# A transformer block on one core: Wo and reciprocal loads over 128 partitions, the last q tile around the shift products, chunk 1's scaling in another order

## Chip, cores and metric

One NeuronCore of a Trainium2 chip. The engines are TensorE (PE), VectorE (DVE), ScalarE (ACT), GpSimd (POOL) and SyncE (SP), which here only issues DMAs. SBUF has 128 partitions, PSUM 8 banks of 128 x 512 float32. The time is the device time of one execution in microseconds (us); the figure given is a median of runs.

## What is computed

A block with adaptive layer norm, linear attention with 32 heads of 32, and a SwiGLU feed-forward part. S = 2048 rows, D = 1024, F = 3584, everything bfloat16. Cut to what matters:

```python
mod = silu(c) @ w_mod                      # six rows of D: sa, ca, ga, sb, cb, gb
h = layernorm(x) * (1 + ca) + sa
q, k, v = split_heads(h @ wqkv)
phi = lambda t: where(t > 0, t + 1, exp(t)) + 1e-06
pq, pk = phi(q), phi(k)
kv = einsum('bhsd,bhse->bhde', pk, v)
z = einsum('bhsd->bhd', pk)
o = einsum('bhqd,bhde->bhqe', pq, kv) / (einsum('bhqd,bhd->bhq', pq, z) + 1e-06)
x = x + ga * (o @ wo)
h = layernorm(x) * (1 + cb) + sb
x = x + gb * ((silu(h @ w_gate) * (h @ w_up)) @ w_down)
```

## The kernel before

The program is one list of operations that the Python code writes out by hand. Each engine runs its own operations in the order in which they were written; a helper (L176) records every operation and works out the semaphore waits between engines from the SBUF bytes and the PSUM banks that each one touches. For PSUM the rule is by whole banks: an operation waits for the last operation of every other engine on its bank. So most lines of the profile carry L176, and instructions are told apart by tile names: `ps` is PSUM, `ht` the transposed and normalised input (two buffers of 8 x 128 x 512), `wqk` the q and k weights, `e`/`rl` and `e1x`/`rlx` the slots for exp and relu, `pqt` and `pkt`/`pk` the finished phi(q) and phi(k), `wo` the output weights, `rb` the reciprocal denominators copied to the partitions of their heads.

The rows of x are worked on in four chunks of 512.

**Chunk 0's q phase** (`q_phase_chunk0`) runs while weights still arrive. Seven of the eight q tiles (nt 0 to 6) grow in seven banks at once, one input tile dt after another (`q_part`), since the scale columns (`mod_sc` with WCA) and shift columns (`mod_sc` with WSA) of the modulation come out of PE in between. For dt 0 to 3 (and dt 4 and 5 in the first seven tiles) the shift isn't added to HT in time; its product with the weights is made separately (`bias_mm`) and added as a bias (`bias_fin` copies it to BIASQ) when ACT takes exp and relu of a tile (`q_phi`). Bank 0 holds those modulation columns, so the eighth tile (nt 7) is made at the end, in bank 0, after `bias_fin`; `h0_shift` then adds the shift to HT for the k products. DVE meanwhile does layer norm statistics of chunk 1 (x tiles 4 to 7; tile 4 by two ACT passes, `act_stats`, and `act_var`), normalises them (`ln1_xn`, `ln1_xn_sum`), and SP sends each through a DMA transpose into HT's second buffer (`th_dma`). `q_min` and `q_add` turn exp and relu into phi(q).

**k groups of chunk 0, then chunks 1 to 3.** `k_group` and `q_group` each make 8 products of 128 x 512 into a bank taken from `next_bank`; `phi_evac` takes exp on ACT, and for each pair of groups `phi_flush` finishes on DVE. `kside` hangs other work behind the k groups of chunk 0: behind group 1 the scaling of chunk 1's HT (`th_mod(1, ...)`, 16 halves of 256 columns) and then the last two q tiles; behind groups 3 and 4 ACT's statistics for tiles 10 and 11.

**G, M and Wo.** For 16 groups `g_group(g)` multiplies phi(k) with the normalised x into five banks (`G_BANKS`); `g_evac` takes a group out on ACT and DVE one group later. Behind g = 0, `z_row` is made, and SP issues ZB's broadcast and the loads of Wo: two calls of `wo_load`, each four DMAs, each with 32 partitions of WO (L938). Behind g = 1, `den` makes the denominators, DVE inverts them into RCB (partition 32 x chunk + head), SP writes them to DRAM in four DMAs, waits, and reads them back in eight DMAs, each filling 32 partitions of RB for four head groups (L988). The first four are awaited together (lane rb0), the next four together (rb1). On DVE `fold_ga` multiplies Wo by ga (g = 6 to 9) and `scale_pq(hg)` multiplies phi(q) by RB (g = 7 to 14), each behind the `g_evac` of its step. `kvt_mm` and `m_mm` form kv and its product with Wo (MW), half 0 behind g = 10 to 12, half 1 after the groups; `wo_part` then multiplies phi(q) by MW. Bank 2 is the bank of G group 14 and also of the first `wo_part`.

The feed-forward part follows and is untouched.

Of the kernel before, what the change touches and what calls it, by code (L numbers as in the profile page):

```python
# [5 lines left out]
FP32 = mybir.dt.float32  # L6
# [256 lines left out]
def bass_adaLN_cond__linear_attn_block__swiglu_ffn__prompt_kernel(  # L263
# [16 lines left out]
    NCH = 4  # L280
# [5 lines left out]
    with ExitStack() as es:  # L286
# [59 lines left out]
        RL = T("rl", 188 * KB, [128, 4, 512], BF16)  # L346
        E1X = T("e1x", 192 * KB, [128, 4, 512], BF16)
        RLX = T("rlx", 196 * KB, [128, 4, 512], BF16)
        ACC = T("acc", 192 * KB, [128, D], FP32)
        MHL = T("mhl", 196 * KB, [128, 2, D], BF16)  # L350
        MHLT = T("mhlt", 192 * KB, [128, 2 * NDT, 128], BF16)
# [351 lines left out]
        def next_bank():  # L703
            i = qk_ctr[0]
            qk_ctr[0] += 1
            return (1, 2, 3, 4, 6, 7, 5, 0)[i % 8] if i < 40 else i % 5 + 1

        def q_group(ch, nt):
            buf, bank = ch % 2, next_bank()
# [39 lines left out]
        def mod_row_b(bank, i, dst):  # L749
# [3 lines left out]
            P.wait_for("sp", [wr])  # L753
            P.dma("mdr%d" % i, dst[:], MDR[i].unsqueeze(0).to_broadcast([128, D]))

        def q_slot(nt):
            return (E1, RL) if nt < 4 else (E1X, RLX)

        def q_phi(nt, bank):
            for buf, fn_ in zip(q_slot(nt), (ACT.Exp, ACT.Relu)):  # L760
                P.act("activation", out=buf[:, nt % 4, :], in_=PS[:, bank, :], func=fn_, bias=BIASQ[:, nt:nt + 1])

        def q_min(nts):
            for nt in nts:
                e = q_slot(nt)[0][:, nt % 4, :]
                P.dve("tensor_scalar", out=e, in0=e, scalar1=1.0, scalar2=1e-6, op0=ALU.min, op1=ALU.add)

        def q_add(nts):
            for nt in nts:
                e, r = q_slot(nt)  # L770
                P.dve("tensor_tensor", out=PQT[:, nt, 0:512], in0=r[:, nt % 4, :], in1=e[:, nt % 4, :], op=ALU.add)

        def q_phase_chunk0():
            qb = [1, 2, 3, 4, 6, 7, 5]
            fin_ca(2, 2)
            for dt in (2, 3):
                h0_first(dt, "dve")
            for nts, dts in ((range(3), (0,)), (range(3), (1,)), ((3, 4, 5, 6), (0, 1))):
                for nt in nts:
                    q_part(nt, qb[nt], dts)  # L780
            for nt in range(7):
                if nt == 4:
                    mod_sc(WCA, 8, range(4, 8))
                    fin_ca(4, 4)
                    for dt in (4, 5):
                        h0_scale_only(dt)
                q_part(nt, qb[nt], (2, 3))
            act_stats(4, (0,))
            for nt in range(7):
                if nt == 6:  # L790
                    mod_sc(WSA, 0, range(6, 8))
                    fin_sa(6, 2)
                    for dt in (6, 7):
                        h0_scale(dt)
                q_part(nt, qb[nt], (4, 5))
            mod_sc(WSA, 0, range(4, 6))
            fin_sa(4, 2, True)
            for dt in (4, 5):
                h0_shift(dt)
            for nt in range(7):  # L800
                if nt == 2:
                    bias_mm((4, 5))
                q_part(nt, qb[nt], (6,))
            for nt in range(7):
                if nt == 1:
                    mod_sc(WSA, 0, range(4), range(4))
                if nt == 3:
                    mod_sc(WSA, 0, range(4), range(4, 8))
                    fin_sa(0, 4, True)
                    ln_ops[1][0]()  # L810
                if nt == 5:
                    bias_mm(range(4))
                    bias_fin()
                q_part(nt, qb[nt], (7,))
            ln_ops[1][1]()
            ln_ops[1][2]()
            ln1_rstd1(5)
            for i, dt in enumerate((4, 5, 0, 1, 2, 3, 6, 7)):
                P.pe("matmul", out=PS[:, 0, :], lhsT=WQK[:, dt, 896:1024], rhs=HT[:, 0, dt, :], start=(i == 0),
                     stop=(i == 7))  # L820
            for dt in range(4):
                h0_shift(dt)
            ln1_xn(5)
            th_dma(5)
            for nt in range(2):
                q_phi(nt, qb[nt])
            act_stats(4, (1,))
            for nt in range(2, 8):
                q_phi(nt, qb[nt] if nt < 7 else 0)
            for f in ln_ops[2]:  # L830
                f()
            act_var(4)
            pool_pow(4)
            for f in ln_ops[3]:
                f()
            ln1_rstd2(6)
            ln1_xn_sum(4)
            th_dma(4)
            q_min((0, 1))
            for st in (6, 7):  # L840
                ln1_xn(st)
                th_dma(st)
            q_add((0, 1))
            for nts in ((2, 3), (4, 5)):
                q_min(nts)
                q_add(nts)
            qk_ctr[0] = 0

        def add(d, k, f):
# [2 lines left out]
        kside = {}  # L852
        ln_ops = [ln1_stats_ops(4 + jj) for jj in range(4)]

        for c0 in (0, 256):
            for dt in range(NDT):
                add(kside, 1, lambda dt=dt, c0=c0: th_mod(1, dt, c0, c0 + 256))
        add(kside, 1, lambda: q_min((6, 7)))
        add(kside, 1, lambda: q_add((6, 7)))
        for jj, k in ((0, 3), (1, 4)):  # L860
            add(kside, k, lambda jj=jj: act_stats(10 + jj))
        q_phase_chunk0()
        for st in range(12, 16):
# [68 lines left out]
        phi_flush()  # L932

        def wo_load(f):
            outs = [WO[32 * g:32 * g + 32, 4 * f:4 * f + 4, :] for g in range(4)]

            def fn(e, outs=outs, f=f):
                return [e.dma_start(out=o_, in_=wov[f, g]) for g, o_ in enumerate(outs)]  # L938

            P.add("sp", fn, reads=[], writes=outs, lane="wo%d" % f, ninc=4, tag="wo")  # L940

        G_BANKS = [0] + [next_bank() for _ in range(4)]

# [26 lines left out]
        def den():  # L970
            for hg in range(NHG):
                for ch in range(NCH):
                    P.pe("matmul", out=PS[32 * ch:32 * ch + 32, 7, :], lhsT=ZSEL[:, hg * 32:hg * 32 + 32],
                         rhs=PQT[:, hg, ch * 512:(ch + 1) * 512], start=(hg == 0), stop=(hg == NHG - 1),
                         skip_group_check=True)
            P.dve("tensor_scalar", out=DEN[:], in0=PS[:, 7, :], scalar1=1e-6, scalar2=None, op0=ALU.add)
            P.dve("reciprocal", out=RCP[:], in_=DEN[:])
            P.dve("tensor_copy", out=RCB[:], in_=RCP[:])
            wr = [P.dma("rdr%d" % ch, RDR[:, ch * 512:(ch + 1) * 512], RCB[32 * ch:32 * ch + 32, :])
                  for ch in range(NCH)]  # L980
            P.wait_for("sp", wr)
            for gh in range(2):
                outs = [RB[32 * hh:32 * hh + 32, 4 * gh:4 * gh + 4, :] for hh in range(4)]
                ins = [RDR.rearrange("(g x) s -> x g s", x=4)[hh, 4 * gh:4 * gh + 4].unsqueeze(0).to_broadcast([32, 4, S])
                       for hh in range(4)]

                def fn(e, outs=outs, ins=ins):
                    return [e.dma_start(out=o_, in_=i_) for o_, i_ in zip(outs, ins)]  # L988

                P.add("sp", fn, reads=[], writes=outs, lane="rb%d" % gh, ninc=4, tag="rb")  # L990

        def scale_pq(hg):
            P.dve("tensor_tensor", out=PQT[:, hg, :], in0=PQT[:, hg, :], in1=RB[:, hg, :], op=ALU.mult)
# [254 lines left out]
```

## Time and profile before

| | us |
|---|---|
| median of 3 runs | 828.01 (827.72 to 828.8) |
| the profiled execution, its own time | 827.71 |
| its span, first to last instruction | 826.0 |
| PE busy in the span | 816.3 |
| DVE busy | 312.2 |
| ACT busy | 197.0 |
| POOL busy | 41.0 |

The granted TensorE clock was 1.000 over the span. A page of the profile gives for each engine the time it was busy, then the chain of work that ended last, then groups of instructions with count, mean duration and the idle time before them, and the DMA issues with the median time from issue to landing. In a timeline a line gives start, duration, engine, operation, the tile written and the tiles read, and in brackets the idle time of the engine before it with what ended it. Matmuls are pipelined: a 128 x 512 one is listed with 379 ns, while the next starts 216 ns after it.

### The profile page before, as it was taken

The page shows a single profiled execution, that of the slowest core. Times are in us where ns is not written, and L with a number is a line of the kernel's source. Part 1 is how long each engine was busy: PE and PEld are TensorE (multiplying, and loading weights), DVE is VectorE, ACT ScalarE, POOL GpSimd, SP SyncE. Part 2 cuts the span into 40 slices and gives each one's busy share as a digit, 9 for nine tenths or more (in the row PEclk, how much of TensorE's full clock was granted, in tenths as well). Part 3 has the DMA queues.
Part 4 walks back from the last instruction along what each step waited for, and adds up shares of the span by engine and source line. Part 5 has one row for each costly group of instructions (what it writes and reads, how often), then busy time and mean ns, then how long its engine had stood idle before and what let it go on. Part 6 is the DMA issues. An engine that isn't in the chain of part 4 may idle for free.

```text
span 826.0 us, 10436 instructions
## 1 busy us (share of the span) xinstructions
PE 816.3 (99%) x4243; PEld 375.9 (46%) x4322; DVE 312.2 (38%) x672; ACT 197.0 (24%) x338; POOL 41.0 (5%) x58
## 2 busy tenths in 40 slices
PE   8999999999999999999999999999999999999998
PEld 4544444444444444444444444444444444444444
DVE  5798988477945521111221112122111111221111
ACT  4758642123341111011111101111110111111011
POOL 1110000000130000020000003000000300000000
DMA  9969756865698995600455570045557004553000
GB/s 316 297 139 223 167 159 149 181 175 211 149 253 245 296 249 153 166 26 26 136 151 151 153 174 25 23 131 153 151 152 182 27 19 126 151 152 88 0 26 26
DMA packets 199392, 119.32 MB, mean 144 GB/s; under 512 B 58024, under 2 KB 183088, under 8 KB 199344
## 3 DMA queue, kind: packets, MB, share of 16 engines
q1 hardware_dynamic: 199328, 118.65, 53.8%
q8 instruction: 34, 0.56, 0.3%
q14 instruction: 14, 0.11, 0.0%
q10 hardware_dynamic: 16, 0.00, 0.0%
HBM read 100.67 MB, written 4.33 MB: 127 GB/s over the span
## 4 chain that ended last, share of the span: by engine, by line
PE 98%; issue 1%; DMA 0%; DVE 0%; POOL 0%; SPq 0%
PE ps L176 98%; DMA xres<-in_A_x_dram 0%; POOL rstd L176 0%; DVE xres L176 0%; DVE stats L176 0%; SPq L176 0%; DVE ht L176 0%; DVE ve L176 0%; DVE mv L176 0%; DVE modcol L176 0%
## 5 line engine op out<-in xcount | busy, mean ns | idle before, releaser
L176 PE MATMUL ps<-h2t,gug 128*128 128x512 bf16 x878 | 210.1, 379 | 0.9
L176 PE MATMUL ps<-h2t,guu 128*128 128x512 bf16 x878 | 209.9, 379 | 0.9
L176 DVE TENSOR_TENSOR at<-sg,ps 128x512 bf16<-128x512 bf16 x112 | 77.0, 687 | 282.8 <-PE ps L176 270.6
L176 ACT ACTIVATE sg<-ps 128x512 bf16<-128x512 f32 x112 | 66.9, 597 | 309.7 <-PE ps L176 298.3
L176 PEld LDWEIGHTS ps<-h2t,guu 128*128 128x128 bf16 x896 | 87.7, 98 | 105.7
L176 PEld LDWEIGHTS ps<-h2t,gug 128*128 128x128 bf16 x896 | 87.6, 98 | 105.5
L176 PE MATMUL ps<-wd_a,at 128*128 128x512 bf16 (+1 forms) x502 | 111.9, 377 | 0.5
L176 PE MATMUL ps<-ht,wqk 128*128 128x512 bf16 x499 | 110.7, 379 | 0.9 <-DVE ht L176 0.2
L176 PE MATMUL ps<-wd_b,at 128*128 128x512 bf16 (+1 forms) x377 | 84.6, 377 | 0.4
L176 PEld LDWEIGHTS ps<-wd_a,at 128*128 128x128 bf16 x512 | 50.1, 98 | 59.6
L176 DVE TENSOR_TENSOR ut<-att,gb_b 128x512 bf16<-128x512 bf16 (+1 forms) x32 | 13.6, 426 | 167.5 <-ACT att L176 167.5
L176 PEld LDWEIGHTS ps<-ht,wqk 128*128 128x128 bf16 x512 | 49.2, 98 | 58.9 <-DVE ht L176 1.0
L176 ACT ACTIVATE att<-ps 128x512 bf16<-128x512 f32 (+1 forms) x32 | 17.4, 591 | 182.1 <-PE ps L176 182.1
L176 PEld LDWEIGHTS ps<-wd_b,at 128*128 128x128 bf16 x384 | 37.6, 98 | 44.7
L176 PE MATMUL ps<-pk,xres 128*128 128x512 bf16 x250 | 55.4, 379 | 0.6 <-issue 0.5
L176 PE MATMUL ps<-mw,pqt 128*128 128x512 bf16 x249 | 55.4, 379 | 0.5 <-issue 0.2
L176 POOL TENSOR_SCALAR h2t<-h2t,modcol 128x512 bf16<-128x512 bf16 x32 | 26.5, 846 | 383.0 <-DMA h2t<-xn 383.0
L176 ACT ACTIVATE e<-ps 128x512 bf16<-128x512 f32 x56 | 33.3, 611 | 31.8 <-PE ps L176 15.8
L176 ACT ACTIVATE junk<-xres 128x1024 bf16<-128x1024 bf16 x26 | 27.6, 1063 | 45.9 <-DVE xres L176 34.2
L176 PEld LDWEIGHTS ps<-mw,pqt 128*128 128x128 bf16 x256 | 24.8, 98 | 30.0 <-issue 0.5
L176 PEld LDWEIGHTS ps<-pk,xres 128*128 128x128 bf16 x256 | 24.6, 98 | 30.1 <-issue 1.3
L176 DVE SCALAR_TENSOR_TENSOR xres<-ps,xres 128x512 bf16<-128x512 f32 x32 | 21.5, 688 | 11.6 <-PE ps L176 11.3
(111 smaller groups left out, 337.8 us busy)
## 6 DMA issues: line engine op xcount, KB each, us to landing
gug<-in_B_w_gate_dram SPq DMA_DIRECT2D x56, 512.0 KB, 4.0
guu<-in_B_w_up_dram SPq DMA_DIRECT2D x56, 512.0 KB, 5.3
xres<-in_A_x_dram SPq DMA_DIRECT2D x20, 256.0 KB, 4.4
rb<-recip_den SPq DMA_DIRECT2D x8, 512.0 KB, 11.7
stgx<-in_w_mod_dram SPq DMA_DIRECT2D x2, 2048.0 KB, 9.3
wd_a<-in_B_w_down_dram SPq DMA_DIRECT2D x4, 1024.0 KB, 7.7
out_dram<-xres SPq DMA_DIRECT2D x31, 128.0 KB, 1.7
xres<-in_A_x_dram SPq DMA_DIRECT2D x3, 1024.0 KB, 6.5
```

The lines of the kernel that those rows point to most:

```text
L176: return getattr(e, method)(**kw)
```

## The change

It has four parts.

1. **DMA shapes.** Each of the eight Wo loads now fills all 128 partitions of one of WO's eight rows instead of 32 partitions of four rows. The DRAM side is an access of [4 groups, 32 rows, 1024]. RCB goes to DRAM in one DMA, whose DRAM side is [4 chunks, 32 heads, 512]. Each of the eight reads of RB fills all 128 partitions of one head group from [4 heads, 32 copies, 2048], and each has a semaphore lane of its own, so that `scale_pq(hg)` waits for its own DMA.
2. **The last q tile.** nt 0 finishes first; ACT copies its bank to QRAW (float32 in SBUF, where the second half of PKT 0 lies later), and nt 7 is made in that bank (1) instead of bank 0. The last shift columns, their `fin_sa`, `bias_mm` and `bias_fin` now stand between the products of nt 7. The q tiles are taken out in the order 1 to 7, then 0 (QORD), and their slots follow that order.
3. **Tile 4 of x** gets both ACT passes together, right behind the copy to QRAW, and its variance, reciprocal root, normalisation and transpose come before those of tile 5; `act_var(4)` stands ahead of `bias_fin` on DVE.
4. **Banks and chunk 1's scaling.** `next_bank` gives bank 0 first and bank 1 last, with a hand-written order for chunk 2. `th_mod(1, ...)` is done in halves for dt 0 to 3 and whole for dt 4 to 7; the last four q tiles are finished behind k group 3; ACT's statistics for tiles 10 and 11 move one group later.

```diff
-            return (1, 2, 3, 4, 6, 7, 5, 0)[i % 8] if i < 40 else i % 5 + 1
+            if i < 24:
+                return (0, 2, 3, 4, 6, 7, 5, 1)[i % 8]
+            if i < 40:
+                return (0, 2, 3, 4, 6, 1, 7, 5, 0, 2, 3, 1, 4, 6, 7, 5)[i - 24]
+            return i % 5 + 1
...
+        QORD = (1, 2, 3, 4, 5, 6, 7, 0)
...
-            act_stats(4, (0,))
...
             for nt in range(7):
-                if nt == 1:
+                q_part(nt, qb[nt], (7,))
+                if nt == 0:
+                    P.act("activation", out=QRAW[:], in_=PS[:, qb[0], :], func=ACT.Copy)
+                    act_stats(4)
+            for i, dt in enumerate(range(NDT)):
+                if i == 1:
                     mod_sc(WSA, 0, range(4), range(4))
-                if nt == 3:
+                if i == 3:
                     mod_sc(WSA, 0, range(4), range(4, 8))
+                    ln_ops[1][0]()
                     fin_sa(0, 4, True)
-                    ln_ops[1][0]()
-                if nt == 5:
+                    ln_ops[1][1]()
+                    act_var(4)
+                    pool_pow(4)
+                if i == 5:
                     bias_mm(range(4))
                     bias_fin()
-                q_part(nt, qb[nt], (7,))
-            ln_ops[1][1]()
+                P.pe("matmul", out=PS[:, qb[0], :], lhsT=WQK[:, dt, 896:1024], rhs=HT[:, 0, dt, :], start=(i == 0),
+                     stop=(i == 7))
             ln_ops[1][2]()
             ln1_rstd1(5)
-            for i, dt in enumerate((4, 5, 0, 1, 2, 3, 6, 7)):
-                P.pe("matmul", out=PS[:, 0, :], lhsT=WQK[:, dt, 896:1024], rhs=HT[:, 0, dt, :], start=(i == 0),
-                     stop=(i == 7))
             for dt in range(4):
                 h0_shift(dt)
+            ln1_xn_sum(4)
+            th_dma(4)
             ln1_xn(5)
             th_dma(5)
...
-        for c0 in (0, 256):
-            for dt in range(NDT):
-                add(kside, 1, lambda dt=dt, c0=c0: th_mod(1, dt, c0, c0 + 256))
-        add(kside, 1, lambda: q_min((6, 7)))
-        add(kside, 1, lambda: q_add((6, 7)))
-        for jj, k in ((0, 3), (1, 4)):
+        for dt, c0, c1 in ([(dt, 0, 256) for dt in range(4)] + [(dt, 256, 512) for dt in range(4)]
+                           + [(dt, 0, 512) for dt in range(4, 8)]):
+            add(kside, 1, lambda dt=dt, c0=c0, c1=c1: th_mod(1, dt, c0, c1))
+        for i in (4, 6):
+            add(kside, 3, lambda i=i: q_pair(i))
+        for jj, k in ((0, 4), (1, 5)):
...
-            outs = [WO[32 * g:32 * g + 32, 4 * f:4 * f + 4, :] for g in range(4)]
+            outs = [WO[:, 4 * f + h, :] for h in range(4)]
...
-                return [e.dma_start(out=o_, in_=wov[f, g]) for g, o_ in enumerate(outs)]
+                return [e.dma_start(out=o_, in_=wov[f, :, :, h, :]) for h, o_ in enumerate(outs)]
...
-            wr = [P.dma("rdr%d" % ch, RDR[:, ch * 512:(ch + 1) * 512], RCB[32 * ch:32 * ch + 32, :])
-                  for ch in range(NCH)]
-            P.wait_for("sp", wr)
-            for gh in range(2):
-                outs = [RB[32 * hh:32 * hh + 32, 4 * gh:4 * gh + 4, :] for hh in range(4)]
-                ins = [RDR.rearrange("(g x) s -> x g s", x=4)[hh, 4 * gh:4 * gh + 4].unsqueeze(0).to_broadcast([32, 4, S])
-                       for hh in range(4)]
+            wr = P.dma("rdr", RDR.rearrange("h (c s) -> c h s", c=NCH), RCB[:])
+            P.wait_for("sp", [wr])
+            for hg in range(NHG):
+                rb_ = RB[:, hg, :]
+                rows = RDR[4 * hg:4 * hg + 4, :].unsqueeze(1).to_broadcast([4, 32, S])
...
-                P.add("sp", fn, reads=[], writes=outs, lane="rb%d" % gh, ninc=4, tag="rb")
+                P.add("sp", fn, reads=[], writes=[RB[:, hg, :]], lane="rb%d" % hg, tag="rb")
```

`q_pair(i)` is `q_min` and then `q_add` of two tiles of QORD.

More of the change, by code (lines that the diff above doesn't have):

```diff
@@ L348, in bass_adaLN_cond__linear_attn_block__swiglu_ffn__prompt_kernel @@
         RLX = T("rlx", 196 * KB, [128, 4, 512], BF16)
+        QRAW = T("qraw", 202 * KB, [128, 512], FP32)
         ACC = T("acc", 192 * KB, [128, D], FP32)
@@ L754, in mod_row_b, with q_phi @@
             P.dma("mdr%d" % i, dst[:], MDR[i].unsqueeze(0).to_broadcast([128, D]))
+        QORD = (1, 2, 3, 4, 5, 6, 7, 0)
         def q_slot(nt):
-            return (E1, RL) if nt < 4 else (E1X, RLX)
-        def q_phi(nt, bank):
+            i = QORD.index(nt)
+            bufs = (E1, RL) if i < 4 else (E1X, RLX)
+            return [t[:, i % 4, :] for t in bufs]
+        def q_phi(nt, src):
             for buf, fn_ in zip(q_slot(nt), (ACT.Exp, ACT.Relu)):
-                P.act("activation", out=buf[:, nt % 4, :], in_=PS[:, bank, :], func=fn_, bias=BIASQ[:, nt:nt + 1])
+                P.act("activation", out=buf, in_=src, func=fn_, bias=BIASQ[:, nt:nt + 1])
         def q_min(nts):
             for nt in nts:
-                e = q_slot(nt)[0][:, nt % 4, :]
+                e = q_slot(nt)[0]
                 P.dve("tensor_scalar", out=e, in0=e, scalar1=1.0, scalar2=1e-6, op0=ALU.min, op1=ALU.add)
@@ L770, in q_add, with q_pair @@
                 e, r = q_slot(nt)
-                P.dve("tensor_tensor", out=PQT[:, nt, 0:512], in0=r[:, nt % 4, :], in1=e[:, nt % 4, :], op=ALU.add)
+                P.dve("tensor_tensor", out=PQT[:, nt, 0:512], in0=r, in1=e, op=ALU.add)
+        def q_pair(i):
+            q_min(QORD[i:i + 2])
+            q_add(QORD[i:i + 2])
         def q_phase_chunk0():
@@ L804, in q_phase_chunk0 @@
             for nt in range(7):
-                if nt == 1:
+                q_part(nt, qb[nt], (7,))
[4 more added lines that the diff above has]
+                if i == 1:
                     mod_sc(WSA, 0, range(4), range(4))
-                if nt == 3:
+                if i == 3:
                     mod_sc(WSA, 0, range(4), range(4, 8))
+                    ln_ops[1][0]()
                     fin_sa(0, 4, True)
-                    ln_ops[1][0]()
-                if nt == 5:
+                    ln_ops[1][1]()
+                    act_var(4)
+                    pool_pow(4)
+                if i == 5:
                     bias_mm(range(4))
                     bias_fin()
-                q_part(nt, qb[nt], (7,))
-            ln_ops[1][1]()
+                P.pe("matmul", out=PS[:, qb[0], :], lhsT=WQK[:, dt, 896:1024], rhs=HT[:, 0, dt, :], start=(i == 0),
+                     stop=(i == 7))
             ln_ops[1][2]()
             ln1_rstd1(5)
-            for i, dt in enumerate((4, 5, 0, 1, 2, 3, 6, 7)):
-                P.pe("matmul", out=PS[:, 0, :], lhsT=WQK[:, dt, 896:1024], rhs=HT[:, 0, dt, :], start=(i == 0),
-                     stop=(i == 7))
             for dt in range(4):
                 h0_shift(dt)
+            ln1_xn_sum(4)
+            th_dma(4)
             ln1_xn(5)
             th_dma(5)
[L825 to L829, printed above, removed]
+            for nt in QORD:
+                q_phi(nt, QRAW[:] if nt == 0 else PS[:, qb[nt % 7], :])
             for f in ln_ops[2]:
                 f()
-            act_var(4)
-            pool_pow(4)
             for f in ln_ops[3]:
@@ L836, in q_phase_chunk0 @@
             ln1_rstd2(6)
-            ln1_xn_sum(4)
-            th_dma(4)
-            q_min((0, 1))
+            q_min(QORD[0:2])
             for st in (6, 7):
@@ L842, in q_phase_chunk0 @@
                 th_dma(st)
[L843 to L846, printed above, removed]
+            q_add(QORD[0:2])
+            q_pair(2)
             qk_ctr[0] = 0
@@ L934, in wo_load @@
         def wo_load(f):
-            outs = [WO[32 * g:32 * g + 32, 4 * f:4 * f + 4, :] for g in range(4)]
+            outs = [WO[:, 4 * f + h, :] for h in range(4)]
             def fn(e, outs=outs, f=f):
-                return [e.dma_start(out=o_, in_=wov[f, g]) for g, o_ in enumerate(outs)]
-            P.add("sp", fn, reads=[], writes=outs, lane="wo%d" % f, ninc=4, tag="wo")
+                return [e.dma_start(out=o_, in_=wov[f, :, :, h, :]) for h, o_ in enumerate(outs)]
+            P.add("sp", fn, reads=[], writes=[WO[:, 4 * f:4 * f + 4, :]], lane="wo%d" % f, ninc=4, tag="wo")
         G_BANKS = [0] + [next_bank() for _ in range(4)]
@@ L978, in den, with fn @@
             P.dve("tensor_copy", out=RCB[:], in_=RCP[:])
-            wr = [P.dma("rdr%d" % ch, RDR[:, ch * 512:(ch + 1) * 512], RCB[32 * ch:32 * ch + 32, :])
-                  for ch in range(NCH)]
-            P.wait_for("sp", wr)
-            for gh in range(2):
-                outs = [RB[32 * hh:32 * hh + 32, 4 * gh:4 * gh + 4, :] for hh in range(4)]
-                ins = [RDR.rearrange("(g x) s -> x g s", x=4)[hh, 4 * gh:4 * gh + 4].unsqueeze(0).to_broadcast([32, 4, S])
-                       for hh in range(4)]
-                def fn(e, outs=outs, ins=ins):
-                    return [e.dma_start(out=o_, in_=i_) for o_, i_ in zip(outs, ins)]
-                P.add("sp", fn, reads=[], writes=outs, lane="rb%d" % gh, ninc=4, tag="rb")
+            wr = P.dma("rdr", RDR.rearrange("h (c s) -> c h s", c=NCH), RCB[:])
[3 more added lines that the diff above has]
+                rows = RDR[4 * hg:4 * hg + 4, :].unsqueeze(1).to_broadcast([4, 32, S])
+                def fn(e, rb_=rb_, rows=rows):
+                    return [e.dma_start(out=rb_, in_=rows)]
+                P.add("sp", fn, reads=[], writes=[RB[:, hg, :]], lane="rb%d" % hg, tag="rb")
         def scale_pq(hg):
```

## The prediction

> **What bounds the kernel now.** I read the page first (busy times, then the chain that ended last), then the waits of PE, then the stretch from 133 to 190 us on SP, DVE and PE, then the DMA issues.
>
> ```profile
> PE 816.3 (99%) x4243; PEld 375.9 (46%) x4322; DVE 312.2 (38%) x672; ACT 197.0 (24%) x338; POOL 41.0 (5%) x58
> ...
> PE 98%; issue 1%; DMA 0%; DVE 0%; POOL 0%; SPq 0%
> ```
>
> PE is busy for 816.3 of 826.0 us and 98% of the chain lies on it. The waits of PE agree:
>
> ```profile
> PE ps L176 <- DMA cs<-in_c_dram: 2.2, 1, 2.2
> PE ps L176 <- issue: 0.6, 4, 0.2
> PE ps L176 <- DVE e L176: 0.2, 1, 0.2
> PE ps L176 <- DVE ht L176: 0.2, 1, 0.2
> ```
>
> After 2.6 us PE loses about 1 us to waits in the whole run. The change neither adds nor drops a product (in both kernels the same rows, in another order), so it can hardly gain: what it can take away is the 0.2 us behind ht. A loss has no such limit. The profiled execution took 827.71 us around its span of 826.0; the median shown is 828.01. I work in span times and add differences to 828.0.
>
> The stretch in which DMAs come nearest to PE is the one behind Wo and the reciprocals. SP issues (start, duration), then DVE (with its idle time before):
>
> ```profile
> 133.94 0.33 SPq L176 DMA_DIRECT2D zb<-z_row  x1
> 134.31 4.40 SPq L938 DMA_DIRECT2D wo<-in_A_wo_dram  x8
> 141.14 1.71 SPq L176 DMA_DIRECT2D recip_den<-rcb  x4
> 149.30 4.02 SPq L988 DMA_DIRECT2D rb<-recip_den  x8
> ```
>
> ```profile
> 153.35 1.28 DVE L176 TENSOR_TENSOR wo<-wo,ga_b 128x1024 bf16<-128x1024 bf16 x2
> 161.28 1.22 DVE L176 TENSOR_TENSOR pqt<-pqt,rb 128x2048 bf16<-128x2048 bf16 x1 [6.65 <-DMA rb<-recip_den]
> 162.42 0.74 DVE L176 SCALAR_TENSOR_TENSOR g<-ps,modcol,gtmp 128x512 bf16<-128x512 f32 x1
> ...
> 180.49 1.21 DVE L176 TENSOR_TENSOR pqt<-pqt,rb 128x2048 bf16<-128x2048 bf16 x1
> 182.62 0.75 DVE L176 SCALAR_TENSOR_TENSOR g<-ps,modcol,gtmp 128x512 bf16<-128x512 f32 x1 [0.92 <-PE ps L176]
> ```
>
> DVE stood 6.65 us for rb, and PE did not notice: five banks of G covered it. But DVE works in order. Behind each scale_pq stands a g_evac, behind the third one the KVT cast that m_mm(0,0) reads on PE at 171.16, and behind scale_pq(7) the eviction of G group 14, whose bank (2) wo_part(0,0) needs. The cover is about 10 us: the first stall comes when rb for hg 2 lands after about 168, the last when that for hg 7 lands after about 184.
>
> **Part by part. The DMAs (Wo, recip_den, rb).** Bytes stay: Wo 8 x 256 KB, recip_den 128 KB, rb 8 x 512 KB. What changes is the shape. Before, each access begins with 32 rows on both sides. After, the SBUF side begins with 128 partitions, but the DRAM side begins with 4: Wo reads [4, 32, 1024], rb reads [4, 32 copies, 2048], recip_den is written as [4, 32, 512]. How many of the 16 DMA engines work on such a transfer? No row of before has sides that differ. The nearest are the three issues of 8 rows:
>
> ```profile
> wo<-in_A_wo_dram SPq DMA_DIRECT2D x8, 256.0 KB, 7.5
> ...
> mod_row<-mr SPq DMA_DIRECT2D x2, 2.0 KB
> ...
> cs<-in_c_dram ACTq DMA_DIRECT2D x1, 2.0 KB
> z_row<-zr SPq DMA_DIRECT2D x1, 4.0 KB
> ```
>
> They alone have no time to landing. In the trace's landing records each has 9 entries, where a DMA of 32 or 128 rows has 16: one written at once and 8 as data lands. So the transfer is shared out along its outermost dimension, 8 rows to 8 engines. I carry this over: 4 outermost on one side, 4 engines. [...]
>
> The rate of an engine has two rows, as DMA traffic of two windows: 173 to 177 us (a load over 128 partitions) and 155 to 169 us (rb, 32 partitions at a time).
>
> ```profile
> DMA packets 774, 1.60 MB, mean 400 GB/s; under 512 B 0, under 2 KB 0, under 8 KB 773
> ```
> ```profile
> DMA packets 815, 2.98 MB, mean 213 GB/s; under 512 B 87, under 2 KB 87, under 8 KB 815
> ```
>
> Over 16 engines that is 25.0 and 13.3 GB/s each. Four engines then move 100 GB/s at best and 53 at worst. Which? They write all 128 partitions, as the fast row, and ask for less than the 213 that even 32 partitions took; but each walks through 32 neighbours of its own, as in the slow row. I take 85, nearer the fast end, and keep both for the range. At 85 GB/s:
> - Wo starts when zb has landed, 133.94 + 4.8 = 138.7 (its row: 4.8 us to landing). 8 x 262144 B / 85 GB/s = 8 x 3.08 = 24.7.
> - recip_den is issued at 141.1 but queues behind Wo: 131072 / 85 = 1.5. SP waits for it as before, with nothing urgent behind.
> - issue and landing of rb: the shortest rb took 4.7 us to landing, of which 512 KB at 213 GB/s are 2.5; leaves 2.2.
> - rb: 8 x 524288 / 85 = 8 x 6.17 = 49.3. The last lands at 138.7 + 24.7 + 1.5 + 2.2 + 49.3 = 216.4.
> - then on DVE scale_pq(7) 1.2 and G's eviction 0.75, on PE the six wo_part products up to kvt_mm(1): 187.26 - 185.87 = 1.4. kvt_mm(1) starts at 219.8 instead of 187.26: +32.5.
>
> The stops begin at m_mm(0,0): rb for hg 2 lands at 138.7 + 24.7 + 1.5 + 2.2 + 3 x 6.17 = 185.6, the KVT cast follows at about 187.6, so PE stands for some 16 us there and again before each m_mm and wo_part. After such a stop PE starts slowly: from 2.61 us the first seven matmuls stood 0.427 us apart, later ones 0.216. Seven times 0.21 is 1.5 us for the last stop (the earlier ones lie inside the waiting); bounds 0 and 3. XRES reloads and stgx1 queue behind rb on those engines, but each share is a sixteenth (2 MB / 16 at 25 GB/s = 5.2 us), before wo_res needs them: no charge, 3 us if late. At 100 GB/s the same sum gives 21.0 + 1.3 + 2.2 + 41.9, rb landed at 205.1, +21.2; at 53 GB/s 39.3 + 2.5 + 2.2 + 78.7, 261.4, +77.5.
>
> **The edits of chunk 0** go together, at -0.2 us. QRAW is one more ACT copy of 0.6 us (row e<-ps, 611 ns) in ACT's idle stretch of 11.5 us before tile 4 lands. The two passes of act_stats(4) follow that landing at 25.55 and end near 27.9 (two at 1.06 and 0.19); act_var and bias_fin stand behind them on DVE. PE, from 23.32: 13 whole products, 16 small, 2, 16, 2, 32, 3, at 0.216 and 0.025 us; the bias products end at 28.6, bias_fin at 29.0, and the first k group needs bank 0 at 29.3. Spare 0.3 us; without it every further us of tile 4 is a us lost. Shifts of HT then end at 30.4, read from 30.2 on one by one, each with 0.4 spare. The scaling of chunk 1 loses four DVE instructions (16 x 0.26 against 8 x 0.26 + 4 x 0.33, 4.2 to 3.4) and starts some 0.4 later, behind the two evictions; the k2 eviction then ends near 45.2 instead of 46.6, when bank 3 is wanted at 46.57. That removes two gaps of PE, 0.04 at 44.67 and 0.13 at 46.76. q_pair(4) and (6) move behind it; the k4 eviction, now near 49.1, is wanted at 50.0. The th transposes on SP go in the order 4, 5, 6, 7 with x12 to x15 behind, 0.3 us earlier than before (SP was busy with th until 39.0). The new bank order leaves at least four groups (6.9 us) between uses; the evictions of those groups ended within 5.5 us of their products. If one failed, its lateness, under 2 us, would be the price.
>
> Sum: 828.0 + 32.5 + 1.5 - 0.2 = **862 us**.
>
> **Rivals.** *Sixteen engines all the same*, the one on the other side: the transfers are shared out by the 128 partitions of SBUF. For it: the bytes and packets are the same, and 128-partition loads run at 400 GB/s. Then Wo takes 5.2, rb 10.5 us, DVE's wait of 6.65 us goes, and PE gains nothing by it since it never felt it: 828.0 - 0.2 = 827.8. Against it: the 9 landings. It decides if rb's hg 2 lands by 168 and hg 7 by 184.
> *Four engines at half rate*: each of the four writes 32 neighbouring partitions in step with another. For it: 213 GB/s where 16 engines shared 32 partitions. Against: 16 engines crowded there, not four. +77.5 + 1.5 - 0.2: 907. [...]
> *Tile 4 late*: bias_fin holds bank 0 and PE; it would have to land 2 us later than 25.5 to cost 1.7 us. 829.7 or more, on top of sixteen engines.
>
> **How the numbers follow.** Four engines between the two rates: 0.58, 845 to 880. Half rate: 0.25. Sixteen engines: 0.15. Tile 4 late: 0.02. The range of 8 in 10 leaves out sixteen engines and some of the far end: 844 to 910. Faster or slower by over 0.2% (1.7 us, about what a measurement of this kernel can tell from no change): slower 0.58 + 0.25 + 0.02 = 0.85; same 0.14; faster 0.01.
>
> **What would show it.** Right: Wo and rb with times to landing in the tens of us or none at all, DMA near a quarter busy from 139 on, DVE waiting for rb several times, PE idle before m_mm(0,0) and before wo_part(0,0) with rb or DVE behind it, the first stop at about 171. The length of one rb, 5.2, 6.2 or 9.8 us apart, tells the rate. Wrong: PE without gaps from 133 to 195 and rb landing by 165; then the time is 827.8 and the carrying over of the 8-row rows to unequal sides was the false step.

## The result, and the profile after

| | before | after |
|---|---|---|
| median, us (run beside each other) | 828.2 | 855.1 (854.48 to 855.82) |
| ratio | | 1.0327, 95% interval 1.0311 to 1.0343 |
| span of the profiled execution | 826.0 | 854.1 |
| granted TensorE clock over the span | 1.000 | 0.988 |

The change costs 27 us. 862 was forecast, with 844 to 910 as the range.

The page of the changed kernel, busy times and the chain that ended last:

```profile
PE 821.6 (96%) x4243; PEld 377.2 (44%) x4322; DVE 312.7 (37%) x668; ACT 197.7 (23%) x339; POOL 40.7 (5%) x58
...
PE 85%; DMA 6%; DVE 3%; ACT 2%; SPq 2%; issue 1%; POOL 0%; ACTq 0%; DVEq 0%
```

PE had 98% of the chain before; now DMA, DVE and SP's queue stand in it. The waits of PE (total us, times, longest) say where:

```profile
PE ps L176 <- DVE g L176: 17.4, 2, 13.7
PE ps L176 <- DVE kvt L176: 3.9, 1, 3.9
...
PE ps L176 <- DVE xres L176: 0.7, 1, 0.7
PE ps L176 <- ACT ht L176: 0.3, 1, 0.3
```

Two waits for G and one for KVT, both written by DVE. DVE itself waits for rb. Its timeline (start, duration, instruction, in brackets the idle time before it and what ended it):

```profile
169.61 1.22 DVE L176 TENSOR_TENSOR pqt<-pqt,rb 128x2048 bf16<-128x2048 bf16 x1 [13.85 <-DMA rb<-recip_den]
170.75 0.74 DVE L176 SCALAR_TENSOR_TENSOR g<-ps,modcol,gtmp 128x512 bf16<-128x512 f32 x1
...
179.60 1.22 DVE L176 TENSOR_TENSOR pqt<-pqt,rb 128x2048 bf16<-128x2048 bf16 x1 [1.90 <-DMA rb<-recip_den]
180.74 0.74 DVE L176 SCALAR_TENSOR_TENSOR g<-ps,modcol,gtmp 128x512 bf16<-128x512 f32 x1
181.40 0.28 DVE L176 CAST kvt<-ps 128x128 bf16<-128x128 f32 x1
...
203.89 1.23 DVE L176 TENSOR_TENSOR pqt<-pqt,rb 128x2048 bf16<-128x2048 bf16 x1 [6.45 <-DMA rb<-recip_den]
205.03 0.75 DVE L176 SCALAR_TENSOR_TENSOR g<-ps,modcol,gtmp 128x512 bf16<-128x512 f32 x1
210.36 1.22 DVE L176 TENSOR_TENSOR pqt<-pqt,rb 128x2048 bf16<-128x2048 bf16 x1 [4.58 <-DMA rb<-recip_den]
211.50 1.40 DVE L176 SCALAR_TENSOR_TENSOR g<-ps,modcol,gtmp 128x512 bf16<-128x512 f32 x2
```

The kernel before had one such wait of 6.65 us, at 161.28. Now all eight scale_pq stand on rb, the last until 210.36, and behind each stands the G eviction or cast that PE needs. PE's timeline answers line by line:

```profile
171.64 0.96 PE L176 MATMUL ps<-g,wv 128*32 128x32 bf16 x100 [3.75 <-DVE g L176]
...
181.74 0.44 PE L176 MATMUL ps<-wo,kvt 32*32 32x512 bf16 x16 [3.90 <-DVE kvt L176]
182.11 5.31 PE L176 MATMUL ps<-pk,xres 128*128 128x512 bf16 x16
...
212.30 1.03 PE L176 MATMUL ps<-mw,pqt 128*128 128x512 bf16 x2 [13.68 <-DVE g L176]
213.56 1.49 PE L176 MATMUL ps<-mw,pqt 128*128 128x512 bf16 x3 [0.22 <-issue]
214.97 1.24 PE L176 MATMUL ps<-g,wv 128*32 128x32 bf16 x128
```

The G eviction that starts at 170.75 lets kvt_mm(0) go on at 171.64, the KVT cast at 181.40 lets m_mm(0,0) start at 181.74, and the evictions from 211.50 on let wo_part(0,0) start at 212.30. The losses exceed the waits because PE also runs slower behind them: the 16 products from 182.11 took 5.31 us, where 16 took 3.68 at 171.52 in the kernel before. The page has the reason in the granted clock, in tenths of full speed for 40 equal slices of the span; the 8 and the 7 stand for 171 to 213 us:

```profile
PEclk9999999987999999999999999999999999999999
```

In the trace's clock records it was 0.50 from 172.55 to 175.97, from 182.79 to 186.21 and from 203.27 to 216.93 us, and 1.00 between and behind them until PE's work was done. PE had stopped at 167.89, 177.84 and 198.62, 4.6 to 5.0 us ahead of each. The products from 212.30 stand 0.43 us apart, twice the usual 0.216. In the three stretches, waits apart, PE's lag behind the kernel before grew by 1.7 (from 4.9 to 6.7), 1.6 (10.6 to 12.2) and 1.7 us (26.4 to 28.1). With the three waits, 21.3 us, that is 26.3 of the 27 us.

Why rb is late, SP's queue and the DMA traffic from 165 to 189 us show:

```profile
135.18 12.83 SPq L948 DMA_DIRECT2D wo<-in_A_wo_dram  x8
148.05 4.41 SPq L176 DMA_DIRECT2D recip_den<-rcb  x1
162.15 24.20 SPq L996 DMA_DIRECT2D rb<-recip_den  x8
186.55 4.77 SPq L176 DMA_DIRECT2D stgx<-in_w_mod_dram  x1
```

```profile
DMA  2222222222222232222222222221224222222222
...
DMA packets 638, 2.56 MB, mean 106 GB/s; under 512 B 20, under 2 KB 20, under 8 KB 636
...
q1 hardware_dynamic: 636, 2.52, 25.6%
```

In the row "DMA" each digit is the busy share of the sixteen engines in tenths. It stands at 2 with nothing else to do but rb: 25.6% is four engines of sixteen. In the landing records of the trace each DMA of Wo, recip_den and rb has 5 entries, one early and 4 later (the first rb, issued at 162.15: 163.10, then 169.12 to 169.59). The first five rb landed at 169.59, 174.58, 179.57, 184.56 and 189.56, 5.0 us apart; then, with stgx1 under way, 195.53, 203.86 and 210.34.

Followed from one PE product to the same one in both traces, PE is 0.6 us late from the first loads on (ahead of every edited instruction), 0.4 behind 47 us, 1.1 behind 73, 4.9 in kvt_mm(0), 10.6 at m_mm(0,0), 12.6 behind m_mm(0,1), 26.4 at wo_part(0,0), 27.7 at kvt_mm(1) and 28.1 at the end.

### The profile page after: what moved, and what is told of

It reads as the page before. It is cut to its first block, busy times and chain, and to the rows that moved or that the text cites. A ratio compares the mean times of both kernels' runs of the same rounds, so it can differ in the third digit from the quotient of the medians.

```text
span 854.1 us, 10429 instructions
## 1 busy us (share of the span) xinstructions
PE 821.6 (96%) x4243; PEld 377.2 (44%) x4322; DVE 312.7 (37%) x668; ACT 197.7 (23%) x339; POOL 40.7 (5%) x58
## 4 chain that ended last, share of the span: by engine, by line
PE 85%; DMA 6%; DVE 3%; ACT 2%; SPq 2%; issue 1%; POOL 0%; ACTq 0%; DVEq 0%
PE ps L176 85%; DMA rb<-recip_den 4%; DMA recip_den<-rcb 2%; SPq L996 2%; DVE pkt L176 1%; DMA xres<-in_A_x_dram 1%; ACT e L176 1%; ACT ht L176 1%; ACT rl L176 1%; DVE ht L176 0%; DVE xres L176 0%; DVE acc L176 0%; DVE e L176 0%; ACT junk L176 0%; DVE stats L176 0%
## 5 line engine op out<-in xcount | busy, mean ns | idle before, releaser
L176 PE MATMUL ps<-mw,pqt 128*128 128x512 bf16 x249 | 56.7, 385 | 14.5 <-DVE g L176 13.7
L176 PE MATMUL ps<-pk,xres 128*128 128x512 bf16 x250 | 58.6, 394 | 0.8 <-issue 0.6
L176 POOL TENSOR_SCALAR h2t<-h2t,modcol 128x512 bf16<-128x512 bf16 x32 | 26.4, 841 | 383.1 <-DMA h2t<-xn 383.1
```

Of the source, the lines that this page charges most:

```text
L176: return getattr(e, method)(**kw)
```

## The experiments

The theory: the DRAM side that begins with 4 puts Wo, recip_den and rb on four engines, and all of the loss comes from rb over DVE to PE. All ratios are to the kernel before, run beside.

| run | rb's DRAM side begins with | rb apart, us | last rb lands | median, us | ratio (95% interval) |
|---|---|---|---|---|---|
| the rest of the change alone | 32, before | 2.4 | 172.05 | 828.71 | 1.0007 (0.9998 to 1.0015) |
| the DMA shapes alone | 4 | 5.0, then 6.5 to 7.5 | 209.24 | 854.72 | 1.0321 (1.0307 to 1.0335) |
| rb undone | 32, before | 2.4, the last 3.5 | 184.47 | 839.1 | 1.0131 (1.0115 to 1.0146) |
| Wo undone | 4 | 5.0, then 5.7 to 8.5 | 197.18 | 842.95 | 1.0180 (1.0166 to 1.0194) |
| rb in pairs | 2 | 10.0, then 11.1 and 12.6 | 248.33 | 893.8 | 1.0791 (1.0775 to 1.0808) |
| stgx1 later | 4 | 5.0, then 6.5 and 5.5 | 207.58 | 853.31 | 1.0303 (1.0289 to 1.0317) |
| rb on sixteen | 16 | 2.2 | 173.61 | 830.06 | 1.0024 (1.0014 to 1.0034) |

**The rest of the change alone.** The three DMA parts of the changed kernel are put back:

```diff
-            outs = [WO[:, 4 * f + h, :] for h in range(4)]
+            outs = [WO[32 * g:32 * g + 32, 4 * f:4 * f + 4, :] for g in range(4)]
...
-            wr = P.dma("rdr", RDR.rearrange("h (c s) -> c h s", c=NCH), RCB[:])
+            wr = [P.dma("rdr%d" % ch, RDR[:, ch * 512:(ch + 1) * 512], RCB[32 * ch:32 * ch + 32, :])
+                  for ch in range(NCH)]
...
-            for hg in range(NHG):
-                rb_ = RB[:, hg, :]
...
+            for gh in range(2):
+                outs = [RB[32 * hh:32 * hh + 32, 4 * gh:4 * gh + 4, :] for hh in range(4)]
...
```

> The changed kernel with Wo, recip_den and rb as before: the edits of chunk 0, the banks and the scaling of chunk 1 alone. Theory (all of the loss comes from the DMAs whose DRAM side begins with 4): 828.2 to 828.9 us. The trace of the changed kernel shows two PE gaps gone (-0.2) and a new wait of 0.74 us near 72 us for an HT block that ACT scales, so some +0.5 against before, within what can be told from no change; SP's rb issue some 4 us long again and the longest wait of DVE for rb near 7 us. Rival (the edits of chunk 0 cost a good part of the 27 us): 835 or more, with PE gaps before 130 us.

828.71, no loss that can be told from none. Its waits of PE name the new one:

```profile
PE ps L176 <- DMA cs<-in_c_dram: 2.2, 1, 2.2
PE ps L176 <- issue: 0.9, 5, 0.2
PE ps L176 <- ACT ht L176: 0.3, 1, 0.3
```

The waits on DVE for G and KVT are gone, and ACT stands ahead of chunk 2's first products.

**The DMA shapes alone**, the same three parts carried into the kernel before:

> The kernel before with the three new DMA shapes alone. Theory: the whole loss, 854 to 855 us, with the new 0.74 us wait near 72 us absent; landings of rb 5.0 us apart for the first five. Rival (the chunk 0 edits share in it, or DMAs and edits only cost together): below 848.

854.72. The two runs together leave nothing for an interplay: the loss is the DMAs'.

**rb undone** and **Wo undone**: the changed kernel with only `rb`, or only `wo_load`, as before.

> The changed kernel with the reads of rb as before (32 partitions each, 32 outermost); Wo and recip_den stay with 4 outermost. Theory: rb is issued at 162 as in the changed kernel, since Wo and recip_den still take the four engines until then, but its halves land 12 and 22 us later as in the kernel before (174, 184). The KVT cast then comes at about 182 instead of 169 and PE stops once, some 10 us, ahead of m_mm(0,0); nothing stops after it. 837 to 842 us. Rival (rb's shape alone is the loss and Wo's only uses up slack): below 831. Rival (Wo's loss is passed on in full): 850 or more.

> The changed kernel with Wo's loads as before; recip_den and rb stay with 4 outermost. Theory: rb is issued near 149 to 150, lands every 5.0 us from 157 on, hg 2 at 167, in time for the KVT cast, so no stop ahead of m_mm(0,0); the sixth to eighth are stretched by stgx1 and the last lands at 192 to 198, against 210 in the changed kernel. One long stop is left, ahead of wo_part(0,0). 836 to 844 us. Rival (the rate of the four engines was set by Wo and rb crowding each other): rb lands faster than every 4 us, below 832.

839.1 and 842.95, both inside. With rb undone PE stops for rb once, 7.8 us, inside kvt_mm(0) and not at m_mm(0,0) as expected; then it waits only 0.5 us for KVT, and 1.4 us at 184.85 for nothing that the profile shows. With Wo undone, rb was issued at 149 instead of 162; there is no early stop, and one of 12.0 us ahead of wo_part(0,0). No wait for Wo itself shows on DVE or PE in the changed kernel: Wo's slowness costs time by pushing rb back by 13 us. There recip_den, issued at 148.05, landed at 162.13, behind the last load of Wo (160.94), and SP issued rb only then (162.15). In both runs the clock was halved from within the long stop until after it (171.90 to 178.72 and 189.95 to 203.60 us; 0.996 and 0.992 over the span).

**rb in pairs.** If four outermost mean four engines, two should mean two. Each head group is read by two DMAs of 64 partitions.

```diff
-                rb_ = RB[:, hg, :]
-                rows = RDR[4 * hg:4 * hg + 4, :].unsqueeze(1).to_broadcast([4, 32, S])
+                outs = [RB[64 * i:64 * i + 64, hg, :] for i in range(2)]
+                ins = [RDR[4 * hg + 2 * i:4 * hg + 2 * i + 2, :].unsqueeze(1).to_broadcast([2, 32, S]) for i in range(2)]
...
```

> The changed kernel, but each read of rb is split in two DMAs of 64 partitions whose DRAM side begins with 2 (two heads, 32 copies, 2048). Bytes, rows and partitions stay. Theory (as many engines as the outermost size): two engines at 25 GB/s, so rb lands every 10.5 us instead of 5.0, the last at 246 to 256 instead of 210, each DMA with 3 landing records; 890 to 902 us. Rival (the limit is SP's issuing, or 128 partitions at a time): 64 partitions each, the same rows; 855 or faster. Rival (each DMA takes engines of its own, so two DMAs of 2 give 4): 855.

893.8, with 3 landing records for each DMA. Its DMA traffic from 165 to 189 us:

```profile
DMA  1111111111111111111112111111111111111111
...
DMA packets 314, 1.26 MB, mean 53 GB/s; under 512 B 9, under 2 KB 9, under 8 KB 313
...
q1 hardware_dynamic: 313, 1.25, 12.8%
```

12.8% is two engines. The bytes, rows and partitions are those of the changed kernel, and rb takes twice as long. Neither SP's issuing nor the partitions set the time here, and the two DMAs of a head group did not get engines of their own: with six issued in that stretch, 12.8% is all they used.

**stgx1 later.**

```diff
-            if g == 10:
-                P.dma("stgx1", STGX[0][:], wmv[:, :, 3072:4096])
...
             P.dma("xr%d" % st, XRES[:, st, :], xv[:, st, :])
+        P.wait_for("sp", [sp7])
+        P.dma("stgx1", STGX[0][:], wmv[:, :, 3072:4096])
```

(sp7 is the instruction of scale_pq(7).)

> The changed kernel with the load stgx1 (2 MB) issued behind the reloads of x and behind scale_pq(7). Theory (stgx1 shares the four engines with the last three rb, which landed 6.0, 8.3 and 6.5 us apart instead of 5.0): those three come 5.0 apart unless the reloads of x (1 MB) meet them, the last at 204.6 to 207, and the time falls by 3 to 6 us, to 849 to 852. stgx1 itself is not late. Rival (the last three are slow for another reason): 855. Rival (stgx1 becomes late for what needs it): above 855.

Faster than the changed kernel, yet 853.31 lies outside the 849 to 852 expected. The sixth rb came 5.0 us behind the fifth, as it should; the seventh and eighth came 6.5 and 5.5 behind, now beside the reloads of x. From the fifth to the last it took 17.0 us instead of 20.8. As the fifth came 1.1 us later in this profile, the last landed at 207.58, 2.8 us earlier, and kvt_mm(1) started 2.8 earlier; 1.0 of that was lost again in PE's products:

```profile
218.70 17.66 PE L176 MATMUL ps<-mw,pqt 128*128 128x512 bf16 x79 [1.00 <-issue]
```

"issue" is a wait for nothing that the profile shows. stgx1 landed at 216.8; a load of instructions (16 KB) started at 216.23 and landed at 217.32, and PE stood from 217.70 on. Whether stgx1 held that load up was not tried here.

**rb on sixteen.** Wo as before; recip_den is kept in four copies, so that the DRAM side of rb has 16 rows:

```diff
-            wr = P.dma("rdr", RDR.rearrange("h (c s) -> c h s", c=NCH), RCB[:])
-            P.wait_for("sp", [wr])
+            wr = [P.dma("rdr%d" % r, RDR.rearrange("(h r) (c s) -> r c h s", r=4, c=NCH)[r], RCB[:]) for r in range(4)]
+            P.wait_for("sp", wr)
...
-                rows = RDR[4 * hg:4 * hg + 4, :].unsqueeze(1).to_broadcast([4, 32, S])
+                rows = RDR[16 * hg:16 * hg + 16, :].unsqueeze(1).to_broadcast([16, 8, S])
```

> As the run with Wo's loads undone, but recip_den is kept four times in DRAM (four writes, each with 4 outermost), so that each read of rb begins with 16 on the DRAM side: 16 rows, 8 copies, 2048, over 128 partitions, the same bytes as in the changed kernel. Theory: 16 engines; the four writes end near 153, rb is issued then and lands every 1.3 us (2.5 at most, if the engines crowd), all by 175, no PE stop: 828 to 829.5 against 842.95. Rival (it is 128 partitions from few DRAM rows that is slow): as without the copies, 843 or more.

rb ran on all engines (the traffic from 157 to 172 us is listed with 103.0% of sixteen, 241 GB/s) and PE no longer waits for DVE: 842.95 falls to 830.06. The median lies 0.6 above the 829.5 expected, and there was a PE stop after all:

```profile
175.00 2.55 PE L176 MATMUL ps<-pk,xres 128*128 128x512 bf16 x11 [1.09 <-issue]
```

A load of instructions (16 KB) started at 172.39, while the last rb was landing, and landed at 173.70; the same one started at 171.04 in the run with the rest of the change alone, where PE did not stop. The stops at 184.85 with rb undone and at 218.70 with stgx1 later fit: each of the three ends 1.3 to 1.4 us after such a load has landed (183.44 and 217.32 in the other two). That PE waits for these loads is an inference from the times.

**Wo as plain rows.** The loads of the kernel before take blocks of 128 rows, and the products swap their two indices:

```diff
-                return [e.dma_start(out=o_, in_=wov[f, g]) for g, o_ in enumerate(outs)]
+                return [e.dma_start(out=o_, in_=A_wo[512 * f + 128 * g:512 * f + 128 * g + 128, :])
+                        for g, o_ in enumerate(outs)]
...
-                         lhsT=KVT[32 * g:32 * g + 32, half, 32 * h:32 * h + 32],
-                         rhs=WO[32 * g:32 * g + 32, 4 * half + h, nh * 512:(nh + 1) * 512], start=True, stop=True,
+                         lhsT=KVT[32 * h:32 * h + 32, half, 32 * g:32 * g + 32],
+                         rhs=WO[32 * h:32 * h + 32, 4 * half + g, nh * 512:(nh + 1) * 512], start=True, stop=True,
```

> The kernel before with Wo read as plain blocks of 128 rows into 128 partitions, which puts head h on partitions 32h (kvt_mm and m_mm swap their two indices to fit); recip_den and rb as before. Theory (128 partitions cost nothing, only the outermost size counts): 16 engines, some 0.7 us for each 256 KB instead of 2.6, Wo landed 4 us earlier than before, rb issued near 145 instead of 149.3, DVE's wait for rb down from 6.65 to some 2.5 us; PE does not notice: 827.5 to 828.6. Rival (128 partitions at a time are the slow thing): Wo lands late as in the changed kernel, 837 or more.

The DMAs did as the theory says: 256 KB every 0.64 to 0.69 us instead of 1.0 to 1.5, rb issued at 146.8, DVE's wait 3.0 us. But the time rose, to 830.77 (ratio 1.0029, interval 1.0018 to 1.0041). One m_mm in the kernel before:

```profile
171.16 0.43 PE L176 MATMUL ps<-wo,kvt 32*32 32x512 bf16 x16
```

and in this run:

```profile
172.18 1.04 PE L176 MATMUL ps<-wo,kvt 32*32 32x512 bf16 x16
```

In the kernel before the 16 products of 32 x 32 read 32 partitions (g) and write 32 partitions (h) in 16 different pairs, and started within 0.05 us. With the indices swapped each writes the partitions with the number of those it reads, only four pairs, and they went in four rounds of 0.22 us: 0.6 us more in each of four m_mm, 2.4 in all. That products of the same pair wait for each other is the author's reading of these times. So the order of rows that makes Wo's DRAM side begin with 4 has a purpose on PE.

**Its loads alone**, with the products of the kernel before:

> The kernel before with Wo's loads as plain blocks of 128 rows, and its products as before. (The rows of Wo thus reach other partitions than the products want; only the time counts.) Theory (the 2.5 us that the run with plain rows of Wo lost come from PE: its 16 small products of m_mm used only the four quarter-arrays with equal row and column, four rounds of 0.22 us instead of one, 0.6 us in each of four m_mm): here they use all sixteen again, so 827.9 to 828.7, with rb issued near 147 and DVE's wait for rb at 3 us. Rival (the loads themselves cost it): 830.8.

828.04, ratio 0.9999 (0.9990 to 1.0008), m_mm back at 0.43 us, DVE's wait for rb 2.9 us. 128 partitions on sixteen engines cost nothing; nor do faster loads gain, since PE never waited for them.

**Wo's rows in another order**, from the run with plain rows:

```diff
-                return [e.dma_start(out=o_, in_=A_wo[512 * f + 128 * g:512 * f + 128 * g + 128, :])
+                return [e.dma_start(out=o_, in_=A_wo[512 * f + 128 * g:512 * f + 128 * g + 128, :].rearrange(
+                    "(b a) n -> a b n", a=8 + 8 * f))
```

> As the run with plain rows of Wo, but the 128 rows of a block are read in another order: the DRAM side begins with 8 (8 strided rows of 16) in the first four loads and with 16 in the last four. (The rows of Wo thus reach other partitions than the products want; only the time counts.) Theory: first four on 8 engines, 1.3 us each, 9 landing records each; last four on 16 engines, 0.7 us each, 16 records; time 828. Rival (any access that is not one plain block is slow): both halves 2.6 us each.

9 records for each of the first four, 16 for each of the last four: the count follows the outermost size at 8 too. The rates are a miss. A 2 KB packet took 84 ns while the first loads were under way (137 to 141 us), as in the changed kernel, but 155 in the middle (142 to 146), when both halves ran together (medians); neither 1.3 nor 0.7 us for a load held over the stretch. A single run, 830.9, like the run with plain rows, whose products it has.

**Scaling of HT earlier**, from the rest of the change alone:

```diff
-        for i, dt in zip([9, 9, 10, 10, 10, 11, 11, 11], range(NDT)):
+        for i, dt in zip([9, 9, 9, 10, 10, 10, 10, 10], range(NDT)):
```

> The run without the DMA shapes, with th_mod(2, dt) for dt 2 and 5 to 7 one group earlier. Theory (the 0.6 us that the rest of the change costs is chunk 2's wait for HT near 72 us, because ACT runs 1.2 us later there): that gap goes, and the time is 827.8 to 828.2 instead of 828.7, the two gaps near 45 us still gone. Rival (moving th_mod up makes evictions late): a new gap between 66 and 80 us, 828.7 or more.

The gap near 72 us is gone from the trace, but the median is 828.59 (ratio 1.0003, 0.9993 to 1.0012): inconclusive in the time. The first products of `wqk` started 0.7 us later in this profile than in that of the kernel before, and between 0.2 us earlier and 1.0 later in those of the other runs, ahead of any edit, which is as much as is at stake.

**Other rows for rb**, from the run with rb on sixteen:

```diff
-                rows = RDR[16 * hg:16 * hg + 16, :].unsqueeze(1).to_broadcast([16, 8, S])
+                rows = A_x[0].rearrange("(r two) d -> r (two d)", two=2)[128 * hg:128 * hg + 128, :]
```

> As the run with 16 outermost for rb, but RB is read from 128 different rows of 4 KB of x instead of 16 rows eight times each. (The denominators thus aren't applied; only the time counts.) In that run a read of 512 KB took 2.18 us, 240 GB/s, where plain 128-partition loads reach 400. Theory (reading the same few rows over and over is what halves the rate): rb lands every 1.3 us, packets of 4 KB take some 160 to 170 ns instead of 274. Rival (16 engines writing 4 KB rows to 128 partitions crowd at the destination): 2.2 us, 274 ns as before. The time, 828 to 830, says little here.

rb landed 1.3 us apart but for one gap of 3.3 us behind the second, 4 KB packets took 159 ns (median); 828.68 (1.0008, 0.9999 to 1.0017), without the PE stop of 1.1 us. The DRAM side here begins with 128 and not with 16, so the packets may also have been dealt out to the engines in another way; that was not separated.

## Why the prediction held, step by step

- *Four outermost, four engines* (carried over from the 8-row DMAs): right. 5 landing records for each DMA, 25.6% of sixteen engines, and with 2 and 8 outermost 3 and 9 records (2: 12.8%). On the other side stood 128 partitions, or 64 with the 2; other unequal pairs below 16 were not tried.
- *85 GB/s*: the term that was mis-sized. It was a choice between rows of 100 and 53, and the fast end is what came: 524288 B in 5.0 us are 105 GB/s. What speaks for it was in the text (the four ask for less than the 213 that sixteen got); the slow row did not carry over. It was taken with sixteen engines at work, where a 4 KB packet took 319 ns; with four it took 159. The sum at 100 GB/s put the last rb at 205.1; the first five at 5.0 us point to 204.6 (189.56 + 3 x 5.0). "Half rate" is out with it: the packet of 4 KB took 159 ns, no more than from 128 different rows on sixteen engines (159, other rows for rb). That the four work in step with one another, as that rival supposed, no run shows.
- *stgx1 and the reloads of x: no charge*: wrong. They were judged by their own lateness at wo_res, and the other side was left out: they share the four engines with rb. Of the 16 landings of stgx1 12 came from 202.40 to 203.58, the other four at 214.26 to 215.24, behind the last rb (210.34). The last three rb came 5.8 us later than at 5.0 us each, and moving stgx1 away shortened that stretch by 3.8 us; 2.0 were left, with the reloads of x under way.
- The two errors work against each other: -11.3 (216.4 to 205.1) for the rate, +5.8 for stgx1. kvt_mm(1) was forecast for 219.8 + 1.5 = 221.3 and came at 214.97, 6.3 early. That 862 lies within 7 us of the result is in part luck: the delay by stgx1 that was left out hid half of what the low rate put too much. With it, at 85 GB/s, the sum would have been 868.
- *From the last landing to kvt_mm(1)*, 1.2 + 0.75 + 1.4 and 1.5 for the slow restart, 4.85: measured 4.63. The six products took 2.67 us instead of 1.39, so the restart cost 1.3, and 0.4 more came behind kvt_mm(1) until the clock was back from 0.50 to 1.00 at 216.93. The text took the slow start from the first seven products (0.427 us apart); the clock, halved behind this stop, it did not name. For those seven the trace of the kernel before has no clock record.
- *First stop at m_mm(0,0)*: wrong by one step. PE stopped at 167.9, inside kvt_mm(0). The cover was read from hg 2 and the KVT cast; but the eviction of G group 7, which kvt_mm(0) reads, stands behind scale_pq(0) on DVE, and that waited until 169.61. Then PE stood 3.9 us at m_mm(0,0) and not some 16, since rb came faster and PE was late already, and no stop followed ahead of the other m_mm of half 0. It changes nothing in the end time, which the last rb sets.
- *The edits of chunk 0, -0.2*: the two gaps did go (PE's lag fell from 0.57 to 0.39 behind 47 us), but a new one of 0.7 us came near 72, where ACT scales HT for chunk 2 and runs 1.2 us later than before (71.77 against 70.57, in the run with the rest of the change alone). The text followed ACT and DVE only to the k4 eviction. In the time it can't be told from nothing.
- *It can hardly gain*: right. No run was clearly faster than the kernel before, not even with the faster loads of Wo (ratio 0.9999).

## What to carry to other kernels

Count the DMA engines from both sides of an access: a tile over 128 partitions read from a DRAM view that begins with 4 ran on four here (25.6% of sixteen). Whoever wants 128 partitions and a permuted order of rows should look for a view whose outermost sizes are among those that ran on sixteen here (16 against 128, 32 or 128 on both sides), or keep the narrower DMAs; and a layout that looks odd on the DMA side may be the one that lets the small products start together (0.43 us for 16 of them, against 1.04 with plain rows). A slow transfer is paid where the last wait behind it ends, so before charging it, list what shares its engines until then. And a stop of PE can cost more than its length: in the changed kernel the clock went to 0.50, 4.6 to 5.0 us after the start of each of the three long ones (3.8, 3.9 and 13.7 us), for 1.6 or 1.7 us of lag more each, though it stayed at 1.00 in the run with a stop of 1.1 us (rb on sixteen).

## What was not expected of the hardware

- Sixteen engines that read 16 rows eight times each moved 240 GB/s over 128 partitions (4 KB packets 274 ns), little more than the 213 of the kernel before; from 128 different rows 400 GB/s (159 ns). So the slow rate of rb in the kernel before need not be due to its 32 partitions; the source, or the way in which the packets are dealt out, counts.
- Wo's loads of 256 KB landed every 1.0 to 1.5 us on 32 partitions, and every 0.64 to 0.69 us on 128 as plain rows. The partitions alone need not be the reason: on 128 partitions with the rows in another order a 2 KB packet took 155 ns in the middle of the loads, as against 84, and the loads on sixteen engines, beside those on eight, landed 1.3 to 2.2 us apart. The two causes were not separated.
- SP's issuing of rb lasted 24.2 us for eight DMAs instead of 4.0: with rb on four engines, the queue that issues stood too. Nothing urgent was behind it here.
